# Last output chunk projected in two halves, with its own buffers and a second store queue, and the whole order planned anew

## The chip, the cores and the metric

The kernel runs on one core of a Trainium2 chip. The metric is the device time of one execution in microseconds (us). A core has five engines that each take their instructions in a fixed order: TensorE (PE, matmuls; its weight loads are listed as PEld), VectorE (DVE), ScalarE (ACT), GpSimd (POOL) and SyncE (SP, which here only issues DMAs). Engines wait for each other by semaphores. PSUM, where matmuls write, has eight banks of 512 fp32 columns.

## The reference

Block-sparse attention (4 batches, 8 heads, 768 positions, head size 64), and a gated long convolution on its output:

```
gate = q . mean of k over each block of 64;  keep the top 3 causal blocks and the own block
attn = softmax(q k^T / 8, kept blocks and causal) v          # per head
x    = heads side by side                                    # [4, 768, 512]
x1, x2, x3 = split(x @ w_proj)                               # w_proj [512, 1536]
c    = irfft(rfft(x2) * rfft(filter))                        # along the 768 positions
out  = (x1 * c * x3) @ w_out                                 # fp32 [4, 768, 512]
```

## The kernel before

Heads are taken in pairs: 16 groups g of two heads, four groups per batch. For each group `prep` transposes k and q on PE (L360, L424), copies them to SBUF (L373 on ACT, L427 on ACT), sums k blocks (L363 on DVE), computes gate scores (L483), the third largest (L493 to L500) and a block mask (L506, L528, L535; for later groups by DMA transposes L462 and L466). `attn` then computes scores in six pieces per group (L558, into two pairs of PSUM banks), exponentials (L565 on ACT), the causal triangle (L570 on POOL), the product with v (L588) and the division (L597, L601 on DVE). The result xn is transposed by DMA (L620) and transformed along the positions by matmuls (L638, L645; copied at L651).

For each batch b, when its four groups are done, `hyena` multiplies the transformed data by w_proj's second part (L747, called s2 here), by the filter's spectrum (L756 on DVE, L766 on POOL), transforms back (L810, copied at L819, combined at L825 on DVE), projects x1 and x3 (L783, called x13 here; x1 is copied by ACT at L789, x1*x3 is formed by DVE at L792), multiplies all (L831 on POOL, into yT), and projects with w_out: for each of six chunks of 128 positions four matmuls (L841), a copy to SBUF (L845, always on ACT in this order) and a store of 256 KB (L848, issued by SP).

The order of all instructions is not written by hand. `build` makes a graph of about 1,600 operations, each with a due time `vt` made of the numbers in `PAR`, and `plan` places them one by one on the engines with a table of costs, buffers (`POOLS`) and PSUM banks; among the operations that are ready within a small margin (`delta`) the earliest due time goes first. Until `warm_until` PE's idle places are filled with matmuls that nobody reads (L945, called fillers here). The result is one fixed list per engine. Any change of a cost, a due time or an operation's count can move everything that comes after.

Of the kernel before, what the change touches and what calls it, by code (L numbers as in the profile page):

```python
# [16 lines left out]
P = 128  # L17
NQ = S // P
NB = S // 64
NP = H // 2  # L20
NG = B * NP
Dm = H * D
# [22 lines left out]
for _pi, _segs in enumerate(PIECES):  # L45
    for (_col, _kc, _q0, _w) in _segs:
        for _c in range(_q0 // P, (_q0 + _w) // P):
# [1 line left out]


PAR = dict(
    direct=2, tm=9, kin=16, p0=-2.69, p1=0.365, pvlag=-6.582, dlag=1.76, dlen=1.383, h0=4.856,
    hlen=3.36, f0=-1.155, f1=7.084, ld=-3.238, s2a=-2.037, s2b=1.216, x0=0.354, x1=1.108, c0=-1.101,
    c1=2.132, o0=1.271, ahead=46.953, delta=0.033, queue=5.995, w0=1.489, wl=1.839, wlag=-9.917, warm_until=32.306,
    tr0=-18.919, trl=6.39, fill0=0.877, v_yT=7.627, v_sd=-1.517, d_k2=6.956, v_trig=-4.154, v_ldq=1.131, v_max=-5.158,
    v_g=0.972, v_Y=0.635, v_k2=0.499, v_rec=-6.814, v_small=-3.021, v_gate=0.152, v_km=0.106, d_x1=3.233, d_shQ=2.566,
    v_xT=-0.742, v_prod=-3.06, v_ldv=0.502, d_yT=8.721, v_ks=0.515, v_osb=-10.289, v_ldk=0.513, v_kT=0.073, v_gT=-1.053,
    d_md=-0.495, d_trig=6.615, v_qT=0.164, v_mT=0.152, v_lt=-2.205, v_fe=7.674, d_eo=-0.025, v_md=-2.102, v_phase=2.124,
    v_shQ=5.115, v_ldf=0.27, d_Y=3.198, v_sel=-7.798, v_warm0=4.967, v_x1=-4.181, v_ldw=0.046, v_tab=0.848, v_va=5.426,
    v_iota=-3.776, d_XT=-0.933, v_qh=0.379, v_h0=4.716, v_eblk=9.913, v_id32=-1.815, v_st=2.29, v_nyq=-4.563, v_s2=-2.561,  # L60
    v_st1=-0.047, v_XT=-3.549, v_t=-1.696, v_ql=-0.667, v_hf=-3.271, d_g=2.878, d_ce=12.21, d_osb=6.098, d_fill=0.038,
    v_w=-6.92, v_ce=0.546, v_fill=7.615, v_op=0.842, v_pv=-3.144, d_w=0.456, v_nrm=4.319, v_ha=-6.505, v_id16=4.506,
    v_eo=3.749, v_x13=-0.318, d_fe=-2.864, v_cv=-2.842, v_sc=0.099, v_T2=-3.366, v_T1=-1.079, d_qh=1.789, v_pq=-5.732,
    d_pq=12.199, v_ex=0.491, v_nid=0.437, a0=0.0, o1=1.0, pen_dve=0.205, late=2.0,
)

POOLS = dict(kn=2, qn=3, vn=2, k2=1, qx=4, ks=2, km=3, m8=2, gs=2, nm=1,
# [1 line left out]
             prod=3, ce=2, sd=2, yT=1, osb=4)  # L69


def c16(n):
    return max(0.026, n / 2400.0 + 0.0025)
# [14 lines left out]

class Graph:
    def __init__(self, par):  # L90
        self.ops, self.par = [], par

    def add(self, tag, vt, eng, emit, rd=(), wr=(), res=(), lock=False, size=0, quad=0):
        o = Op()
        vt += self.par.get("v_" + tag, 0.0)
        o.i, o.tag, o.vt, o.eng, o.emit, o.lock, o.size = len(self.ops), tag, vt, eng, emit, lock, size
        o.quad = quad
        deps = set()

        def norm(xs):  # L100
            return [x if isinstance(x, tuple) else (x, 0) for x in xs]

        bufs = []
        for b, p in norm(rd):
            deps.update(b.w.get(p, ()))
            b.r.setdefault(p, []).append(o)
            bufs.append(b)
        for b, p in norm(wr):
            deps.update(x for x in b.w.get(p, ()))
            deps.update(x for x in b.r.get(p, ()) if x is not o)  # L110
            b.w.setdefault(p, []).append(o)
            bufs.append(b)
        deps.discard(o)
        o.deps = list(deps)
        o.bufs = list({id(b): b for b in bufs}.values())
        for b in o.bufs:
            b.left += 1
        o.alloc = list({id(b): b for b in o.bufs + list(res)}.values())
        self.ops.append(o)
        return o  # L120


def pe_cost(mms):
    occ = sum(mms)
    return occ, occ + 0.23


def dve(n, rate=1.0):
    occ = n / (960.0 * rate) + 0.074
    return occ, occ + 0.15  # L130


def act(n, sb=False):
    occ = n / 1200.0 + 0.058 + (0.09 if sb else 0.0)
    return occ, occ + 0.165


def pol(occ):
    return occ, occ + 0.11


def build(par):
    g_ = Graph(par)
    add = g_.add
    C = {}

    def cb(name):
        if name not in C:
            C[name] = Buf(None)
        return C[name]  # L150

    def psb(n=1):
        return Buf("sp" if n == 2 else "bk")
# [4 lines left out]
    def e_id(E, nc, en):  # L158
# [4 lines left out]
        rd=[cb("id32")], wr=[cb("id16")])  # L163

    add("nid", T0 + 2.05, {"DVE": dve(64)}, lambda E, nc, en: nc.vector.tensor_scalar_mul(E.nid, E.id32, -float(S)),
        rd=[cb("id32")], wr=[cb("nid")], lock=True)
# [51 lines left out]
    for i in range(POOLS["kt"]):  # L218
# [5 lines left out]
        def e_fk(E, nc, en, i=i):  # L224
            eng = nc.vector if en == "DVE" else nc.gpsimd
            for h in range(2):
# [7 lines left out]
                rd=[cb("eblk")], wr=[(cb(("slot", i)), 1)], lock=True)])  # L234
# [13 lines left out]
    for t in range(HC):  # L248
        for hf in range(2):
            vt = par["tr0"] + par["trl"] * (0.33 * t + 0.16 * hf)  # L250
# [27 lines left out]

    kn, qn, va = {}, {}, {}
    for g in range(NG):  # L280
        b, j = divmod(g, NP)
        vt = g + par["ld"]
        kn[g], qn[g], va[g] = Buf("kn"), Buf("qn"), Buf("va")

        for n_, (src, dst) in enumerate((("k", kn[g]), ("q", qn[g]))):
            for t in range(2):
                def e_ld(E, nc, en, b=b, j=j, t=t, dst=dst, src=src, g=g):
                    nc.sync.dma_start(E.sb(dst)[:, :, 1 - t if src == "q" and g >= par["tm"] else t, :],
                                      getattr(E, src)[b, 2 * j + t].rearrange("(c p) d -> p c d", p=P))
                add("ld" + src, vt + .02 * n_ + .01 * t, {"SP": (0.5, 0)}, e_ld, wr=[(dst, t)], size=270)  # L290
        vn = Buf("vn")

        def e_lv(E, nc, en, b=b, j=j, vn=vn):
            s_ = E.v[b, 2 * j:2 * j + 2].rearrange("t (c p) d -> p (t c) d", p=P)
            nc.sync.dma_start(E.sb(vn), s_)

        def e_va(E, nc, en, vn=vn, va=va[g]):
            nc.gpsimd.affine_select(out=E.sb(va).rearrange("p t c d -> p (t c) d")[:, :, 0:D],
                                    in_=E.sb(vn), compare_op=ALU.is_ge, fill=0.0, base=0,
                                    pattern=[[0, 2 * NQ], [0, D]], channel_multiplier=0)  # L300

        add("ldv", vt + .6, {"SP": (0.55, 0)}, e_lv, wr=[vn], size=540)
        add("va", g + par["p0"] + 1.0, {"POOL": pol(0.86)}, e_va, rd=[vn, cb("small")], wr=[va[g]])

    fts = []
    for t in range(HC):
        f0, f1 = Buf("t"), Buf("t")
# [416 lines left out]
    def hyena(b):  # L724
        last = b == B - 1
        a, L = NP * b + par["h0"], par["hlen"]

        def v(f, lo=None, hi=None):
            if lo is not None:
                f = par[lo] + (par[hi] - par[lo]) * f  # L730
            return a + L * f
# [4 lines left out]
        for c in range(HC):  # L736
            for kind in range(2):
# [5 lines left out]
                def e_s2(E, nc, en, c=c, kind=kind, xa=xa):  # L743
# [8 lines left out]
                    wr=[xa], res=[ta, tb, Y])  # L752
                for i, dst in enumerate((ta, tb)):
                    def e_t(E, nc, en, c=c, kind=kind, i=i, dst=dst, xa=xa):
# [3 lines left out]
                        rd=[xa, (cb("HA"), c), (cb("HB"), c), cb("HA0")], wr=[dst])  # L758
            (t1, t4), (t3, t2) = ts[(c, 0)], ts[(c, 1)]
            for kind, (x, y, op) in enumerate(((t1, t2, ALU.subtract), (t3, t4, ALU.add))):  # L760
                for p_ in ((0,) if c < 2 else (0, 1)):
                    def e_y(E, nc, en, c=c, kind=kind, x=x, y=y, op=op, p_=p_):
# [6 lines left out]
                        rd=[x, y], wr=[(Y, (c, kind, p_))], lock=True)  # L769
        yT = Buf("yT")  # L770
        prods = {}
        for dc in range(NP):
            prod = prods[dc] = Buf("prod")
            for hf in range(2):
                cs = slice(HS * hf, HS * (hf + 1))
                x1 = Buf("x1")
                for m in range(2):
# [9 lines left out]
                    def e_xe(E, nc, en, cs=cs, m=m, xq=xq, x1=x1, prod=prod):  # L787
# [6 lines left out]
                    vt = v(f, "x0", "x1")  # L794
                    add("x13", vt, {"PE": pe_cost([c16(HS)] * 4)}, e_x,
                        rd=[xT[g] for g in gs] + [(cb(("wp", 2 * m)), c_) for c_ in range(NP)], wr=[xq], res=[x1, prod])
# [4 lines left out]
        for dc in range(NP):  # L801
            prod = prods[dc]
            ce, sd = Buf("ce"), Buf("sd")
            for p_ in range(2):
# [3 lines left out]
                def e_cv(E, nc, en, dc=dc, p_=p_, cv=cv):  # L808
# [4 lines left out]
                vt = v(f, "c0", "c1")  # L813
                need = [(Y, (p_, 0, 0)), (Y, (p_, 1, 0)), (Y, (2, 0, p_)), (Y, (2, 1, p_))]
                add("cv", vt, {"PE": pe_cost([c16(HS)] * 3)}, e_cv,
                    rd=need + [(cb("G"), 3 * p_ + n_) for n_ in range(3)], wr=[cv], res=[ce, sd, yT])
# [5 lines left out]
                else:  # L822
                    for i, op in enumerate((ALU.add, ALU.subtract)):
# [5 lines left out]
                        def e_yt(E, nc, en, i=i, dc=dc, sd=sd, prod=prod):  # L829
# [2 lines left out]
                                E.sb(yT)[:, dc, cs], E.sb(prod)[:, cs], E.sb(sd)[:, cs])  # L832
                        add("yT", vt + .04, {"POOL": pol(0.955), "DVE": dve(HS)}, e_yt, rd=[(prod, i), (sd, i)],
                            wr=[(yT, (dc, i))], lock=True)
        for c in range(NQ):
            op_, osb = psb(), Buf("osb")
            vt = v(c / 6.0, "o0", "o1")

            def e_op(E, nc, en, c=c, op_=op_):
                for d2 in range(NP):  # L840
                    nc.tensor.matmul(E.bk(op_), lhsT=E.sb(yT)[:, d2, P * c:P * (c + 1)], rhs=E.wo[:, d2, :],  # L841
                                     start=(d2 == 0), stop=(d2 == NP - 1))

            def e_os(E, nc, en, op_=op_, osb=osb):
                (nc.vector.tensor_copy if en == "DVE" else nc.scalar.copy)(E.sb(osb), E.bk(op_))  # L845

            def e_o(E, nc, en, c=c, osb=osb):
                nc.sync.dma_start(E.out[b, P * c:P * (c + 1), :], E.sb(osb))  # L848

            add("op", vt, {"PE": pe_cost([c16(Dm)] * 4)}, e_op,  # L850
                rd=[(yT, (d2, c // HC)) for d2 in range(NP)] + [(cb("wo"), c_) for c_ in range(NP)], wr=[op_], res=[osb])
            add("osb", vt + .02, {"ACT": act(Dm), "DVE": dve(Dm)}, e_os, rd=[op_], wr=[osb])
            add("st", vt + .04, {"SP": (0.5, 0)}, e_o, rd=[osb], size=262)


    for g in range(NG):
        C[("slots", g)] = Buf(None)
        C[("slots", g)].w[0] = sum(slot_init[:min(g + 1, POOLS["kt"])], [])
    for g in range(NG):
        prep(g)  # L860
    for g in range(NG):
        attn(g)
    filt()
    for b in range(B):
        hyena(b)
    return g_.ops

# [298 lines left out]
```

## Time and profile before

| | |
|---|---|
| median of 4 runs | 233.94 us (233.21 to 234.58) |
| profiled execution | 234.22 us, of which the span of the profile is 232.5 us |
| PE busy | 223.7 us (96%), 2189 matmuls, 116 of them fillers |
| DVE, ACT, POOL busy | 184.1, 176.0, 168.9 us |
| PE busy from 101 to 224 us | 123.00 of 123.00 us |
| last matmul ends | 228.8 us |
| last output copy | 228.89 us, 0.59 us long |
| last store issued | 229.5 us |
| stores, issue to landing | 2.0 us at least, 2.3 in the median |
| granted TensorE clock | 0.998 |

The page's rows name an engine, a line of the kernel, the operation and tiles as out<-in with partitions x elements; `x24 | 14.2, 590` means 24 instructions, 14.2 us busy in sum, 590 ns on the average. "idle before <-releaser" is the time for which the engine stood idle ahead of that group, and who ended it. Ends of matmuls are modelled, so a row of matmuls is better timed from start to start than by its end.

### The profile page before, as it was taken

Reading aid. Unit: us, or ns where it says so; the run is one execution under the profiler, and the core shown is the slowest. Engines: PE = TensorE matmul, PEld = TensorE weight load, DVE = VectorE, ACT = ScalarE, POOL = GpSimd, SP = SyncE. Lnnn points to the kernel's source line nnn. Section 1 sums busy time; section 2 is a strip of 40 time slices with the busy share of each in tenths; the row PEclk is TensorE's granted clock in tenths of the full one; section 3 lists DMA queues with packets and bytes.
Section 4 is the critical chain, followed back from the end, with each engine's and each line's share of the span. In section 5 each row is a group of like instructions: output and inputs, shape, how many; then the busy total and the mean of one; then the engine's idle time right before and its main releaser. Section 6 shows DMA issues by size and latency. Waiting matters only on the chain.

```text
span 232.5 us, 6222 instructions
## 1 busy us (share of the span) xinstructions
PE 223.7 (96%) x2189; PEld 151.4 (65%) x2189; DVE 184.1 (79%) x615; ACT 176.0 (76%) x295; POOL 168.9 (73%) x309
## 2 busy tenths in 40 slices
PE   8999999999897999999999999999999999999993
PEld 5787786767665677667655677676556667545551
DVE  7999779788987989998899597887987856594730
ACT  2988999999987798899957887999376675405343
POOL 8156467798669799979699999774598666069760
PEclk9999999999999999999999999999999999999999
DMA  7999999999999999999999999959912310512015
GB/s 157 330 223 202 218 176 233 231 209 253 180 218 234 220 213 200 222 252 223 174 227 215 284 190 226 174 98 178 259 52 79 70 34 3 171 45 90 3 45 226
DMA packets 120223, 40.91 MB, mean 176 GB/s; under 512 B 114304, under 2 KB 114304, under 8 KB 120192
## 3 DMA queue, kind: packets, MB, share of 16 engines
q1 hardware_dynamic: 120192, 40.51, 88.9%
q8 instruction: 17, 0.28, 0.6%
q14 instruction: 14, 0.11, 0.2%
HBM read 24.64 MB, written 6.29 MB: 133 GB/s over the span
## 4 chain that ended last, share of the span: by engine, by line
PE 63%; DVE 5%; DMA 4%; ACT 3%; issue 2%; SPq 1%; DVEq 0%; ACTq 0%
PE ps L783 15%; PE ps L558 10%; PE ps L841 9%; PE ps L747 7%; PE ps L588 6%; PE ps L810 6%; PE ps L638 4%; DMA t<-in_moe_w_proj_dram 2%; DMA kn<-in_k_dram 2%; PE ps L360 2%; PE ps L645 2%; ACT ex L565 2%; DVE ks L363 1%; PE ps L483 1%; DVE qx L457 1%
## 5 line engine op out<-in xcount | busy, mean ns | idle before, releaser
L565 ACT ACTIVATE ex<-ps 128x1024 f16<-128x1024 f32 (+1 forms) x96 | 86.4, 925 | 16.7 <-PE ps L558 16.1
L570 POOL TENSOR_SCALAR_AFFINE_SELECT ex<-ex 128x256 f16<-128x256 f16 x96 | 40.0, 424 | 23.3 <-ACT ex L565 21.5
L558 PE MATMUL ps<-qt,kt 76*128 76x512 f16 (+7 forms) x256 | 50.5, 305 | 1.2 <-ACT ex L565 0.7
L783 PE MATMUL ps<-xT,wp 128*128 128x384 f16 x256 | 49.8, 325 | 0.0
L766 POOL TENSOR_TENSOR Y<-t,t 128x512 f16<-128x512 f32 (+1 forms) x32 | 40.3, 1266 | 11.3 <-DVE t L756 10.2
L831 POOL TENSOR_TENSOR yT<-prod,sd 128x384 f16<-128x384 f32 x32 | 32.3, 1021 | 3.6 <-DVE sd L825 2.3
L373 ACT CAST kt<-ps 64x384 f16<-64x384 f32 x64 | 30.1, 472 | 6.1 <-PE ps L360 4.0
L558 PEld LDWEIGHTS <-kt 76*128 76x128 f16 (+1 forms) x256 | 23.5, 97 | 15.8 <-issue 1.8
L783 PEld LDWEIGHTS <-wp 128*128 128x128 f16 x256 | 24.1, 97 | 14.5 <-issue 0.3
L588 PEld LDWEIGHTS <-ex 128*128 128x128 f16 x672 | 25.5, 97 | 3.4 <-issue 1.0
L588 PE MATMUL ps<-va,ex 128*128 128x65 f16 x672 | 26.7, 193 | 0.5 <-DVE prod L792 0.3
L789 ACT CAST x<-ps 128x384 f16<-128x384 f32 x32 | 15.3, 478 | 14.0 <-PE ps L783 12.4
L792 DVE TENSOR_TENSOR prod<-ps,x 128x384 f32<-128x384 f32 x32 | 17.6, 552 | 8.6 <-PE ps L783 8.1
L841 PE MATMUL ps<-wo,yT 128*128 128x512 f16 x96 | 23.3, 379 | 0.0
L747 PE MATMUL ps<-wp,XT 128*128 128x512 f16 x96 | 22.5, 379 | 0.1
L845 ACT COPY osb<-ps 128x512 f32<-128x512 f32 x24 | 14.2, 590 | 8.2 <-PE ps L841 7.9
L651 DVE CAST XT<-ps 128x256 f16<-128x256 f32 (+1 forms) x30 | 16.1, 544 | 5.5 <-PE ps L645 3.6
L945 PE MATMUL ps<-warm 128*128 128x256 f16 x116 | 18.5, 296 | 1.1 <-DVE warm L1133 1.1
L810 PE MATMUL ps<-G,Y 128*128 128x384 f16 x96 | 19.0, 326 | 0.0
L363 DVE TENSOR_REDUCE ks<-ps 128x6 f32<-128x384 f32 x32 | 17.3, 547 | 2.2 <-ACT kt L373 1.4
L601 DVE TENSOR_TENSOR xn<-ps,rec 128x384 f16<-128x384 f32 x32 | 17.6, 551 | 0.7
L825 DVE TENSOR_TENSOR sd<-ce,ps 128x384 f32<-128x384 f32 x32 | 16.3, 546 | 1.6 <-ACT ce L819 1.5
(107 smaller groups left out, 376.8 us busy)
## 6 DMA issues: line engine op xcount, KB each, us to landing
kn<-in_k_dram SPq DMA_DIRECT2D x32, 192.0 KB, 4.4
vn<-in_v_dram SPq DMA_DIRECT2D x16, 384.0 KB, 5.5
qn<-in_q_dram SPq DMA_DIRECT2D x32, 192.0 KB, 4.5
out_dram<-osb SPq DMA_DIRECT2D x24, 256.0 KB, 2.3
t<-in_moe_w_proj_dram SPq DMA_DIRECT2D x12, 256.0 KB, 4.1
t<-in_moe_filter_fft_dram SPq DMA_DIRECT2D x6, 256.0 KB, 4.5
qt<-qx SPq DMA_DIRECT2D x14, 96.0 KB, 3.9
t<-in_moe_w_out_dram SPq DMA_DIRECT2D x4, 256.0 KB, 3.6
```

Source lines behind the costliest of these rows:

```text
L363: nc.vector.reduce_sum(E.sb(ks)[:, 6 * hf:6 * hf + 6], E.bk(kp)[:, 0:HS].rearrange("p (n t) -> p n t", t=64), axis=AX.X)
L373: (nc.scalar.copy if en == "ACT" else nc.vector.tensor_copy)(E.sb(Kt[g])[r, HC * hf:HC * (hf + 1), 1 - t, :], E.bk(kp)[r, 0:HS].rearrange( ...
L558: nc.tensor.matmul(o[:, col:col + w], lhsT=E.sb(Kt[g])[0:KR[t], kc, 1 - t, :], rhs=E.sb(Qt[g])[0:KR[t], q0 // P:(q0 + w) // P, 1 - t, :], ...
L565: nc.scalar.activation(E.sb(ex)[:, 0:w], E.sp(sp)[:, 0:w], AF.Exp, scale=ESC)
L570: nc.gpsimd.affine_select(out=dv, in_=dv, compare_op=ALU.is_ge, fill=0.0, base=0, pattern=[[0, 2], [1, P]], channel_multiplier=-1)
L588: nc.tensor.matmul(o[:, 65 * c:65 * c + 65], lhsT=E.sb(exs[pi])[:, col:col + P], rhs=E.sb(va[g])[:, t, kc, :], start=(kc == 0), stop=(kc = ...
L747: nc.tensor.matmul(E.bk(xa), lhsT=w, rhs=E.wp[:, j, Dm:2 * Dm], start=(j == 0), stop=(j == NP - 1))
L766: (nc.vector if en == "DVE" else nc.gpsimd).tensor_tensor(E.sb(Y)[ro, n_, :], E.sb(x)[ri, :], E.sb(y)[ri, :], op=op)
L783: nc.tensor.matmul(E.bk(xq)[:, 0:HS], lhsT=E.wp[:, d2, 2 * Dm * m + P * dc:2 * Dm * m + P * (dc + 1)], rhs=E.sb(xT[gs[d2]])[:, cs], start= ...
L810: nc.tensor.matmul(E.bk(cv)[:, 0:HS], lhsT=E.sb(Y)[:, 3 * p_ + n_, P * dc:P * (dc + 1)], rhs=E.G[:, 3 * p_ + n_, :], start=(n_ == 0), stop ...
L831: (nc.vector if en == "DVE" else nc.gpsimd).tensor_mul(E.sb(yT)[:, dc, cs], E.sb(prod)[:, cs], E.sb(sd)[:, cs])
L841: nc.tensor.matmul(E.bk(op_), lhsT=E.sb(yT)[:, d2, P * c:P * (c + 1)], rhs=E.wo[:, d2, :], start=(d2 == 0), stop=(d2 == NP - 1))
```

## The change

The output projection of the last batch is rewritten. Chunks 0 to 4 remain four matmuls of 512 columns, one copy and one store of 256 KB. Chunk 5 becomes two operations of 256 columns each, with four matmuls, one copy and one store of 128 KB apiece; the store of the second half is issued by ACT (`nc.scalar.dma_start`) instead of SP. In the last batch chunks 4 and 5 are copied into buffers of the pool `prod`, not of `osb`. The chunks' due times in the last batch follow the order 0 to 5, where the order before came out as 2, 1, 5, 4, 3, 0.

`Graph` can now add a number per operation and group to the due time (`v_<tag>_<group>`), some 390 such numbers are set, and most of the old numbers in `PAR` have other values. `POOLS` and the cost functions are as before. So the plan comes out differently on every engine.

```diff
@@ PAR
-    direct=2, tm=9, kin=16, p0=-2.69, p1=0.365, pvlag=-6.582, dlag=1.76, dlen=1.383, h0=4.856,
+    direct=2, tm=9, kin=16, p0=-2.688, p1=0.365, pvlag=-7.248, dlag=1.795, dlen=1.312, h0=4.884,
...
+    d_pq=12.713, v_ex=0.48, v_nid=0.704, v_va_0=0.132, v_ldq_1=-0.543, v_ldq_2=1.495, v_ldv_3=0.132, v_ldk_4=-0.165, v_ldq_4=-0.2,
...
@@ class Graph
-        self.ops, self.par = [], par
+        self.ops, self.par, self.group = [], par, -1
...
         vt += self.par.get("v_" + tag, 0.0)
+        if self.group >= 0:
+            vt += self.par.get("v_%s_%d" % (tag, self.group), 0.0)
@@ hyena
-        for c in range(NQ):
-            op_, osb = psb(), Buf("osb")
-            vt = v(c / 6.0, "o0", "o1")
+        for c, n0, n1 in [(c, 0, Dm) for c in range(NQ - last)] + [(NQ - 1, 0, 256), (NQ - 1, 256, Dm)] * last:
+            op_, osb, n = psb(), Buf("prod" if last and c >= 4 else "osb"), n1 - n0
+            vt = v(0.0, "o0", "o1") + 0.01 * (c + n0 / Dm) if last else v(c / 6.0, "o0", "o1")
...
-                    nc.tensor.matmul(E.bk(op_), lhsT=E.sb(yT)[:, d2, P * c:P * (c + 1)], rhs=E.wo[:, d2, :],
-                                     start=(d2 == 0), stop=(d2 == NP - 1))
+                    nc.tensor.matmul(E.bk(op_)[:, 0:n1 - n0], lhsT=E.sb(yT)[:, d2, P * c:P * (c + 1)],
+                                     rhs=E.wo[:, d2, n0:n1], start=(d2 == 0), stop=(d2 == NP - 1))
...
-                (nc.vector.tensor_copy if en == "DVE" else nc.scalar.copy)(E.sb(osb), E.bk(op_))
+                (nc.vector.tensor_copy if en == "DVE" else nc.scalar.copy)(E.sb(osb)[:, 0:n], E.bk(op_)[:, 0:n])
...
-                nc.sync.dma_start(E.out[b, P * c:P * (c + 1), :], E.sb(osb))
+                (nc.scalar if n0 else nc.sync).dma_start(E.out[b, P * c:P * (c + 1), n0:n1], E.sb(osb)[:, 0:n1 - n0])
...
-            add("op", vt, {"PE": pe_cost([c16(Dm)] * 4)}, e_op,
+            add("op", vt, {"PE": pe_cost([c16(n)] * 4)}, e_op,
...
-            add("osb", vt + .02, {"ACT": act(Dm), "DVE": dve(Dm)}, e_os, rd=[op_], wr=[osb])
-            add("st", vt + .04, {"SP": (0.5, 0)}, e_o, rd=[osb], size=262)
+            add("osb", vt + .02, {"ACT": act(n), "DVE": dve(n)}, e_os, rd=[op_], wr=[osb])
+            add("st", vt + .04, {"SP": (0.5, 0)}, e_o, rd=[osb], size=262 * n // Dm)
...
     for g in range(NG):
+        g_.group = g
         prep(g)
     for g in range(NG):
+        g_.group = g
         attn(g)
+    g_.group = -1
     filt()
     for b in range(B):
+        g_.group = b
         hyena(b)
```

What the plan makes of it, read from the two built programs: PE's list is the same for its first 283 matmuls (the profile before has the 283rd at 32 us) and has one filler more (117); its score pieces then stand at the same place, counted in PE's work, to within 1.5 us until piece 63 of 96, and drift up to 4.6 us from there. SP's list differs first at its fourth issue: the first two filter loads go ahead of both halves of the first q load, where they stood between the halves. ACT's list differs first after 52 instructions. All copies of output chunks stay on ACT.

## The prediction

> **What bounds the kernel now.** I read the page's first part, then PE by stretches, then the stretches where it idles, then the end. The page says that PE is the bound:
>
> ```profile
> PE 223.7 (96%) x2189; PEld 151.4 (65%) x2189; DVE 184.1 (79%) x615; ACT 176.0 (76%) x295; POOL 168.9 (73%) x309
> ```
>
> An average hides where the 4% lie, so the next view is busy time by stretches. Look at the PE column only:
>
> ```profile
> core 0: us, PE busy (x) PEld busy (x) DVE busy (x) ACT busy (x) POOL busy (x), PEclk, DMA share, GB/s
> 33.00:60.00 27.00, 25.75 (x336) 19.17 (x335) 22.92 (x102) 26.67 (x44) 20.28 (x46) 1.00 1.17 221
> 60.00:80.00 20.00, 17.61 (x198) 11.90 (x197) 17.60 (x62) 16.98 (x28) 15.92 (x30) 1.00 1.18 208
> 95.00:101.00 6.00, 5.67 (x55) 3.87 (x54) 5.71 (x20) 4.86 (x9) 5.00 (x9) 1.00 1.31 206
> 101.00:224.00 123.00, 123.00 (x1150) 79.46 (x1148) 97.29 (x294) 84.51 (x136) 93.54 (x157) 1.00 0.69 141
> 224.00:229.00 5.00, 4.81 (x23) 1.98 (x21) 0.28 (x1) 3.04 (x6) 1.05 (x2) 1.00 0.49 188
> ```
>
> From 101 to 224 us PE never idles, and the clock is full. No order can be faster there, only slower. What an order can win lies at 33 to 101 us: 1.25 + 2.39 + 0.33 = 4.0 us by these rows. Ends of matmuls are modelled, so busy time swallows short waits. Counted from start to start (24 matmuls of 512 columns in 5.18 us, so 216 ns each; 16 of 384 columns in 2.60 us, 163 ns each) PE loses 7.8 us there, spread over two dozen places of 0.1 to 0.85 us. The largest cluster:
>
> ```profile
> 71.27 1.02 PE L747 MATMUL ps<-wp,XT 128*128 128x512 f16 x4
> 72.99 0.85 PE L360 MATMUL ps<-id,kn 128*128 128x128 f32 x6 [0.69 <-DMA kn<-in_k_dram]
> 75.74 0.44 PE L528 MATMUL ps<-id,nm 128*128 128x128 f16 x5 [0.65 <-DVE ks L363]
> 76.57 1.02 PE L747 MATMUL ps<-wp,XT 128*128 128x512 f16 x4
> ```
>
> A load of k is late by 0.7 us, then a PSUM bank that DVE still reads, by 0.65. The end is short:
>
> ```profile
> 223.45 5.36 PE L841 MATMUL ps<-wo,yT 128*128 128x512 f16 x24
> 228.03 0.59 ACT L845 COPY osb<-ps 128x512 f32<-128x512 f32 x1 [0.32 <-PE ps L841]
> 228.89 0.59 ACT L845 COPY osb<-ps 128x512 f32<-128x512 f32 x1 [0.28 <-PE ps L841]
> DMA to landing us min/median/max: 2.0/2.3/4.7
> ```
>
> 24 projection matmuls end at 228.81, the last copy runs to 229.48, its store is issued at 229.5 and lands 2.0 us later, and 1.0 us of closing work ends the span at 232.5. Only these 3.7 us after the last matmul belong to the edit that can be read in the diff.
>
> **The change part by part**, against the profiled execution (234.22 us, span 232.5, so 1.72 around it). It lies 0.28 above the median of 233.94, and the sum is lowered by that at the end.
>
> *The tail.* Eight matmuls of 256 columns replace four of 512: three of 256 take 0.33 us elsewhere (L638, 109 ns each), so 8 x 109 = 872 against 4 x 216 = 864 ns: nothing. Copies cost by size:
>
> ```profile
> L845 ACT COPY osb<-ps 128x512 f32<-128x512 f32 x24 | 14.2, 590 | 8.2 <-PE ps L841 7.9
> L819 ACT COPY ce<-ps 128x384 f32<-128x384 f32 x16 | 7.6, 479 | 3.3 <-DVE sd L825 1.6 <-PE ps L810 1.5
> ```
>
> 128 columns less save 111 ns, so 256 columns take some 368 ns. But chunk 4's copy and both halves stand one after the other on ACT: chunk 4 from 228.03 to 228.62, the first half, ready at 228.46, until 228.99, the second, ready at 228.89, until 229.36 instead of 229.48. That is -0.12, not -0.22. The last store moves 128 KB instead of 256. No row shows a lone store of that size; at the most that any slice of the page moved (330 GB/s) the missing 128 KB are 0.4 us, at least they are nothing; I take -0.2. That ACT issues it removes a hop of 0.02 us (copy end to SP's issue). ACT's queue is not used before; SP's stores took 332 to 1301 ns to issue, so this costs nothing to +0.97, and I take nothing, since that queue is empty. Nothing is queued behind it on ACT. Tail: -0.3, ends -0.5 to +0.85.
>
> The row that bears on it: a store of 256 KB lands here 2.0 us after its issue. The page "DMA: Bandwidth & Descriptors" of the Trainium skill speaks against this part. Under "Anatomy of one DMA" (written of GpSimd's path) it gives a DMA about 2.0 us whatever its size plus its bytes at 436 GB/s, 2.6 us for such a store, and under "Rules for kernel authors" it says that spreading DMAs over several issuing engines saves only issue time. By it the half store would gain an estimated 0.3 us and the second queue no more than an issue; the sum would then be 0.1 us lower.
>
> *Own buffers, chunk order.* A copy reuses the first of four `osb` buffers four chunks (4 x 0.86 = 3.4 us) later, and its store has landed 0.59 + 2.05 us after that copy began: no wait before, none to win. The `prod` buffers' last readers are multiplies (L831) that PE must await anyway. Chunks 0, 1, 2 first means that the second half of yT is wanted one chunk later. PE idles 0.19 us in 224 to 229: -0.1, ends -0.19 and 0.
>
> *The plan, 0 to 33 us.* PE's list is the same. The first q half is issued two places later, but q's transpose needs both halves, and the second keeps the seventh place: nothing. The one added filler (109 ns) comes just ahead of PE's waits for exponentials: covered; 0.11 if that cover is gone.
>
> *33 to 60 us.* ACT is busy 26.67 of 27.00 us. The new order swaps copies with exponentials (up to 1.1 us of ACT work either way) but has the same ACT work ahead of exponential 24, so the stretch ends with ACT: 0, ends -0.33 and +0.5 (half the largest swap, if ACT is then starved once).
>
> *60 to 80 us.* PE's list is the same up to the gate after L528. The late k load keeps its place behind the same issues (the transpose of xn goes ahead of three issues that it followed): its 0.7 us stay. Then ACT's list changes: a weight cast (L322, 0.61) moves ahead of three k copies (L373, 0.47 each), and an exponential goes behind that cast and one more copy. The mask transpose (L528) now waits for x1's copy in its bank, which ends after two casts, two k copies and itself: 73.62 + 2 x 0.61 + 3 x 0.47 = 76.25 instead of 75.74. Then the second matmul group of s2 (0.86 us) is pulled forward to where x13 had waited, and by score piece 37 I come to 81.2 us with 0.3 us less work done, against 81.54 before. +0.1; ends -1.1 (the 0.65 and, from start to start, 0.30 and 0.19 behind it gone) and +1.1 (the ACT work that now stands ahead of the exponential).
>
> *95 to 101 us.* Same PE and DVE lists; one k copy goes behind an exponential. 0, end -0.33.
>
> *101 to 224 us.* Much is moved: batch 0's projection comes together, k transposes go 11 us later, loads change places with stores on SP. SP's queue is where stores wait for ACT with loads behind them. Counting PE work between producer and consumer, the transposed scores' masks (gate to scores) get more room (10.5 us at least before, 13.5 now), the filter products 5.6 to 6.3, the multiplies ahead of w_out about the same. Closer are bank waits on DVE in batch 1: one x13 group loses 1.7 us of PE work ahead of it while the L825 that frees its bank gets 2.1 us more DVE work; the timeline has 3.4 us of room there, so -0.4. With DVE at 97 of 123 us I take +0.3. It can't be below 0; the upper end is 2.4, what PE lost in 60 to 80, the worst stretch that this planner left.
>
> Sum: -0.3 - 0.1 + 0 + 0 + 0.1 + 0 + 0.3 = 0.0, so 234.2 for an execution like the profiled one and **233.9** for the median. A comparison of this kernel can tell about 0.5% from no change, 1.17 us: same means 232.8 to 235.1.
>
> **The rivals.** *New waits in the dense part (slower).* The place is 110 to 195 us, where the new order differs most; the mechanism is a matmul that waits for DVE or POOL to free a bank. For it: DVE is at 97 of 123 us and 33 to 101 us shows that such plans do leave such waits. Against it: the distances above. Four waits of the 0.65 seen at L528 are 2.6 us: 233.94 + 2.6 - 0.4 = 236.1. It decides from 1.6 us of new PE idle on.
>
> *The early waits close (faster).* If the three waits from L528 on go (1.1) and half the 0.33 at 95 to 101, with the tail's 0.4 and no new wait: 233.94 - 0.4 - 1.1 - 0.2 = 232.2. For it: 4.0 us of idle PE. Against it: the lists there are nearly the same, and two of the causes are untouched.
>
> *The split does nothing.* The halves' copies queue on ACT and the landing is latency: then the tail gives 0.1 and the time is 234.1, inside the forecast's class.
>
> **How the numbers follow.** Forecast, the split's failure with it: 0.57. Slower by the rival: 0.23. Faster: 0.20. The forecast's own range is 232.8 to 235.1; to hold 8 in 10 it reaches about half into each rival: 232.3 to 235.6.
>
> **What would show it.** Right: PE busy within 0.5 us of 123 between 101 us and the last 5 us; the last copies near 0.37 us each; from the last matmul to the span's end 3.4 us. Wrong: idle PE over 1.5 us after 101 us; PE's wait at L528 gone; a last store that lands over 2.3 us after its issue.

## The result: 0.5% slower, and the profile after

| | before | after |
|---|---|---|
| median of all runs | 233.84 us (68 runs) | 235.12 us (42 runs) |
| ratio to the kernel before, 95% interval | 1 | 1.0051 (1.0039 to 1.0064) |
| profiled execution, and its span | 234.22, 232.5 us | 235.40, 233.7 us |
| last matmul starts / last store lands | 228.43 / 231.56 us | 229.83 / 232.74 us |

The forecast was "same", 233.9 us. The measured time lies inside the range of 232.3 to 235.6, but the change is 1.2 us in the direction that was given 0.23.

The same view as before, busy time by stretches, shows where PE stands idle now (first number: length; second: PE busy; then PEld, DVE, ACT, POOL, PEclk):

```profile
33.00:60.00 27.00, 24.84 (x336) 19.13 (x333) 22.28 (x100) 26.70 (x44) 21.93 (x49) 1.00 1.19 219
60.00:80.00 20.00, 17.39 (x188) 11.64 (x185) 17.16 (x62) 16.24 (x28) 15.76 (x27) 1.00 1.07 207
95.00:101.00 6.00, 5.72 (x58) 4.02 (x56) 5.71 (x21) 5.22 (x10) 5.15 (x9) 1.00 1.29 188
101.00:124.00 23.00, 23.00 (x221) 14.56 (x219) 20.89 (x69) 17.69 (x28) 18.95 (x40) 1.00 1.20 236
124.00:132.00 8.00, 6.90 (x94) 5.25 (x93) 6.98 (x13) 5.58 (x10) 6.77 (x13) 1.00 1.10 242
132.00:225.00 93.00, 93.00 (x837) 59.43 (x836) 72.71 (x216) 59.65 (x98) 66.00 (x104) 1.00 0.58 107
```

Ahead of 101 us the picture is nearly the old one: from 33 to 60 us PE is busy for 0.9 us less, but counted from start to start (the time between two matmul starts, less what the first needs) it lost the same there to within 0.2 us. Behind it PE was full before; now 1.10 us are missing from 124 to 132 us, and nowhere else. The view of PE's waits from 100 to 140 us has a single line for the kernel after, and none for the kernel before (us in total, times, longest):

```profile
PE ps L686 <- DVE eo L674: 1.1, 1, 1.1
```

PE's timeline around that place:

```profile
126.38 0.50 PE L408 MATMUL ps<-id,kn 128*128 128x128 f32 x3
127.98 0.50 PE L686 MATMUL ps<-F,eo 128*128 128x256 f16 x3 [1.10 <-DVE eo L674]
```

From start to start it is 1.27 us. L686 is the transform of group 8's xn along the positions; it reads `eo`, the sum and the difference of xn's halves, made by DVE. DVE's timeline, and then POOL's, say why `eo` is late:

```profile
123.47 0.55 DVE L649 TENSOR_TENSOR xn<-ps,rec 128x384 f16<-128x384 f32 x1
124.64 0.56 DVE L411 TENSOR_REDUCE ks<-ps 128x6 f32<-128x384 f32 x1 [0.62 <-PE ps L408]
125.11 1.47 DVE L505 SCALAR_TENSOR_TENSOR qx<-qn,qx 128x640 f16<-128x640 f32 x1
126.51 1.89 DVE L674 TENSOR_TENSOR eo<-xn 128x384 f16<-128x384 f16 x2
129.25 0.67 DVE L699 CAST XT<-ps 128x512 f16<-128x512 f32 x1
```

```profile
125.12 0.78 POOL L618 TENSOR_SCALAR_AFFINE_SELECT ex<-ex 128x256 f16<-128x256 f16 x2
125.99 1.72 POOL L814 TENSOR_TENSOR Y<-t,t 64x512 f16<-64x512 f32 x1
```

Two things are to be seen. The order: xn comes at 123.47, behind a block of twelve filter products (L804, from 115.95 to 123.55), where the kernel before had it at 116.26, in front of them. DVE's rows of the kernel before:

```profile
116.26 0.56 DVE L601 TENSOR_TENSOR xn<-ps,rec 128x384 f16<-128x384 f32 x1
122.31 1.79 DVE L457 SCALAR_TENSOR_TENSOR qx<-qn,qx 128x640 f16<-128x640 f32 x1
124.03 0.55 DVE L626 TENSOR_TENSOR eo<-xn 128x384 f16<-128x384 f16 x1
130.17 0.20 DVE L597 RECIPROCAL rec<-ps 128x6 f32<-128x6 f32 x1 [2.19 <-PE ps L483]
```

And the durations: the two `eo` take 1.89 us, qx 1.47, while the views of single lines give these spreads over the kernel (ns, least/median/most):

```profile
L674 DVE TENSOR_TENSOR eo<-xn x19: 341/354/1443, 62.0 to 200.4; 128x384 f16<-128x384 f16 x19
```

```profile
L505 DVE SCALAR_TENSOR_TENSOR qx<-qn,qx x7: 817/925/1470, 91.0 to 160.7; 128x640 f16<-128x640 f32 x7
```

```profile
L840 DVE TENSOR_TENSOR prod<-ps,x x32: 537/552/559, 84.8 to 225.0; 128x384 f32<-128x384 f32 x32
```

eo and qx read two operands from SBUF, and their longest take 4 and nearly 2 times as long as their shortest; prod reads one of its two from PSUM and does not vary. The first eo (126.51 to 127.92) ends 0.2 us after POOL's Y ends (127.71), and Y itself takes 1.72 us instead of 1.29 (the Y before it): it is recorded from 125.99, while qx ran until 126.58. By these rows each holds the other up; for eo, run 2 below tests it.

The Trainium skill's page "SBUF — State Buffer", section "Who interferes with whom", says that a VectorE instruction with two SBUF inputs contends with a GpSimd instruction that reads SBUF, and that the ports which the two engines share are an exclusive lock. These rows agree: the long eo lasted until Y had ended.

The end of the kernel by the timeline, ACT's copies and the issues of the stores, and then the copies by their line:

```profile
229.32 1.25 ACT L894 COPY prod<-ps 128x512 f32<-128x512 f32 x3 [0.33 <-PE ps L890]
229.93 0.81 SPq L898 DMA_DIRECT2D out_dram<-prod  x2
230.60 0.38 ACTq L898 DMA_DIRECT2D out_dram<-prod  x1
```

```profile
L894 ACT COPY prod<-ps x3: 372/377/586, 229.3 to 230.2; 128x256 f32<-128x256 f32 x2, 128x512 f32<-128x512 f32 x1
```

The copies are 0.37 us long, as forecast. ACT's store is issued at 230.60 and lands at 232.74, 2.14 us later; the whole chunk took 2.06.

### The profile page after: what moved, and what is told of

The parts are those of the page before. It is cut to its first block, busy times and chain, and to the rows that moved or that the text cites. A ratio compares the mean times of both kernels' runs of the same rounds, so it can differ in the third digit from the quotient of the medians.

```text
span 233.7 us, 6234 instructions
## 1 busy us (share of the span) xinstructions
PE 222.1 (95%) x2194; PEld 151.0 (65%) x2194; DVE 186.7 (80%) x616; ACT 174.8 (75%) x296; POOL 168.6 (72%) x308
## 4 chain that ended last, share of the span: by engine, by line
PE 67%; ACT 11%; DMA 8%; DVE 6%; issue 3%; POOL 2%; SPq 1%; DVEq 0%; ACTq 0%
PE ps L831 15%; PE ps L606 9%; PE ps L890 9%; PE ps L795 7%; PE ps L858 6%; PE ps L636 6%; ACT ex L613 5%; DMA kn<-in_k_dram 4%; DMA xT<-xn 4%; PE ps L686 3%; ACT kt L421 3%; PE ps L999 3%; PE ps L408 2%; PE ps L693 2%; ACT qx L475 1%
## 5 line engine op out<-in xcount | busy, mean ns | idle before, releaser
L831 PEld LDWEIGHTS <-wp 128*128 128x128 f16 x256 | 24.1, 97 | 13.8
L837 ACT CAST x<-ps 128x384 f16<-128x384 f32 x32 | 15.4, 480 | 13.4 <-PE ps L831 12.5
L890 PE MATMUL ps<-wo,yT 128*128 128x512 f16 (+1 forms) x100 | 23.5, 370 | 0.0
L411 DVE TENSOR_REDUCE ks<-ps 128x6 f32<-128x384 f32 x32 | 17.4, 548 | 4.4 <-PE ps L408 2.4
L894 ACT COPY osb<-ps 128x512 f32<-128x512 f32 x22 | 12.9, 585 | 10.1 <-PE ps L890 10.0
L804 DVE TENSOR_TENSOR t<-ps,HA 128x512 f32<-128x512 f32 x24 | 16.4, 683 | 2.4 <-PE ps L795 2.2
```

What stands on the lines that cost most here:

```text
L831: nc.tensor.matmul(E.bk(xq)[:, 0:HS], lhsT=E.wp[:, d2, 2 * Dm * m + P * dc:2 * Dm * m + P * (dc + 1)], rhs=E.sb(xT[gs[d2]])[:, cs], start= ...
L890: nc.tensor.matmul(E.bk(op_)[:, 0:n1 - n0], lhsT=E.sb(yT)[:, d2, P * c:P * (c + 1)], rhs=E.wo[:, d2, n0:n1], start=(d2 == 0), stop=(d2 == ...
```

## The experiments

The theory to be tested: the 1.2 us are lost by PE at 124 to 132 us to DVE, and the tail is worth about 0.1 us. Rivals: the tail itself costs the time; or the new order is tight in many places, so that no single wait can be blamed. In most runs the planned order of the kernel after is kept and a few operations are moved by hand: `move` takes the named operations (tag and running number in the graph; group 8 has eo16 and eo17) out of the list and puts them elsewhere, so that all other instructions keep their places. Of the tags, `sel` is a triangle mask and `Y` a product on POOL; `ql` is qx, `nrm` xn, `t` a filter product and `XT` a copy on DVE; `T` is the DMA transpose of qx's result, and `ldk` a load of k.

### 1. eo ahead of qx on DVE

```diff
     order = plan(PAR)
+    order = move(order, ["eo16", "eo17"], ahead="ql21")
```

> The kernel after, with two instructions of DVE's list moved: group 8's sum and difference (eo, L674) go ahead of the qx instruction (L505) that stood before them. One-wait theory: the 1.2 us are PE's wait at 128 us for these two eo; they now begin at 125.1 instead of 126.5 and end before PE wants them at 126.9, the wait goes, PE loses nothing in 124 to 132 us, and the time falls by 1.0 to 1.3 to about 233.9, ratio to the kernel before 1.000 (0.998 to 1.002). Spread theory (the new order is tight everywhere): another wait of 0.5 us or more comes up behind it and the ratio stays at 1.003 or more. Tail theory (the halves and ACT's queue cost it): nothing changes, 1.005.

Measured: 1.0070 (1.0047 to 1.0092). PE's wait for eo was gone, the time was not. In the profiled execution PE's clock was at half for 3.4 us from 58.3 us on (rows in the last section), and at 111 us PE was 1.6 us later than in the kernel after, so this profile says little by itself. But 8 of the 12 executions had a granted clock of 0.999 or more, and their median is 235.7 us too. It was run again (5).

### 2. Y two places later on POOL

```diff
+    order = move(order, ["Y13"], behind="sel59")
```

> The kernel after, with one instruction of POOL's list moved: the product Y (L814, 1.72 us long) that began at 125.99 goes behind the two triangle masks (L618) that followed it. DVE's and PE's lists stay. If an eo with both operands in SBUF is held by a long POOL instruction beside it (eo took 1.41 us there, 0.35 in the median, and ended 0.2 us after Y), the first eo now takes 0.35 to 0.5 us, both end at 127.2 or before instead of 128.0, PE's wait shrinks from 1.1 to 0.2 to 0.5 us, and the ratio to the kernel before falls from 1.005 to about 1.002. If eo is slow for a reason of its own (its place behind qx), it still takes over 1 us and the ratio stays at 1.005. If the tail makes the loss, 1.005 as well, but with the short eo.

Measured: 1.0016 (0.9994 to 1.0038); 234.61 us, against 235.34 for run 3 on the same chip, which has the same order without this move. The interval lies just below that of the kernel after (1.0039 to 1.0064) and overlaps that of run 3. DVE's timeline, and then POOL's:

```profile
124.62 1.47 DVE L505 SCALAR_TENSOR_TENSOR qx<-qn,qx 128x640 f16<-128x640 f32 x1
126.01 0.61 DVE L674 TENSOR_TENSOR eo<-xn 128x384 f16<-128x384 f16 x2
```

```profile
124.64 0.77 POOL L618 TENSOR_SCALAR_AFFINE_SELECT ex<-ex 128x256 f16<-128x256 f16 x2
128.26 1.27 POOL L814 TENSOR_TENSOR Y<-t,t 64x512 f16<-64x512 f32 x1
```

No instruction of DVE or PE was touched, and the two eo, with nothing of POOL beside them, take 0.61 us instead of 1.89. qx stays at 1.47: the two masks still run beside it. PE's wait fell from 1.27 to 0.20 us, and another of 0.31 us appeared at 135.7 us. What a DVE instruction costs is decided here by what POOL does beside it.

### 3 and 4. The tail undone, and the tail alone

Run 3 is the kernel after with the last chunk whole:

```diff
             def e_op(E, nc, en, c=c, op_=op_, n0=n0, n1=n1):
+                if n0:
+                    return
+                n1 = Dm
...  (the same in e_os and e_o: the first half does the whole chunk, the second nothing; SP stores)
```

> The kernel after with its order, but with the last chunk whole again: four matmuls of 512 columns, one copy, one store of 256 KB by SP (own buffers and chunk order stay). One-wait theory: the wait at 128 us stays and the tail is worth 0.1 us (from the last matmul's start to the span's end 4.07 us before and 3.88 after, less 0.11 of matmul length), so 235.2 to 235.4, ratio 1.0055 to 1.0065. The prediction's tail of -0.3: 235.4. Tail theory: the loss goes, 233.9, ratio 1.000.

Run 4 is the kernel before, in its own order, with its last chunk in halves:

```diff
+                if b == B - 1 and c == 0:
+                    for n0, s_ in ((0, op_.slot), (256, E.other)):
+                        for d2 in range(NP):
+                            nc.tensor.matmul(E.ps[:, 512 * s_:512 * s_ + 256], lhsT=E.sb(yT)[:, d2, 0:P],
+                                             rhs=E.wo[:, d2, n0:n0 + 256], start=(d2 == 0), stop=(d2 == NP - 1))
+                    return
...
+                    nc.sync.dma_start(E.out[b, 0:P, 0:256], E.t["prod"][2][:, 0:256])
+                    nc.scalar.dma_start(E.out[b, 0:P, 256:Dm], E.t["prod"][0][:, 0:256])
```

> The kernel before with its order, with the new tail alone: its last chunk projected, copied and stored in halves, the second half's store by ACT's queue. One-wait theory: -0.1 us, ratio 0.9995 (0.998 to 1.001). The prediction's tail: -0.3, ratio 0.9987. Tail theory: +1.2, ratio 1.005.

Measured: run 3 1.0053 (1.0028 to 1.0078), run 4 1.0004 (0.9977 to 1.0030). Neither moves its kernel measurably: the tail is not the cause. The profiles give its worth, from the end of the last matmul (its start plus 216 or 109 ns) to the landing of the last store: 2.91 us before and 2.90 in run 3 (whole), 2.80 after and 2.81 in run 4 (halves). That is 0.1 us.

### 5. The kernel after, and run 1, once more

> The kernel after once more, as the yardstick for the others. One-wait theory: the wait of 1.1 to 1.3 us for eo at 128 us is in this profile too, since nothing random stands ahead of it, and the ratio to the kernel before is 1.005 (1.003 to 1.007). If the wait was an accident of one execution, PE loses under 0.5 us between 124 and 132 us here.

> The first experiment (eo ahead of qx on DVE) once more. Its profile had PE's wait at 128 us gone, but 1.7 us more lost ahead of 101 us, where its instructions are those of the kernel after, and a granted clock of 0.97 and 0.96 from 33 to 80 us. One-wait theory with a disturbed first run: ratio 0.999 to 1.002, no PE loss in 124 to 132 us, and 11.5 to 12.5 us lost ahead of 101 us by the stretches (PE start to start) instead of 13.6. If the move itself costs time, the ratio is again 1.005 or more.

Measured: the kernel after 1.0044 (1.0017 to 1.0071), run 1's edit 1.0058 (1.0029 to 1.0087). The loss is in the kernel after's second profile too (0.85 us in front of L693, which reads the second eo). With eo moved ahead it is not gone but elsewhere; PE's waits from 100 to 140 us in that run:

```profile
PE ps L831 <- DVE prod L840: 0.4, 1, 0.4
PE ps L831 <- DVE XT L699: 0.3, 1, 0.3
```

These are banks that DVE frees later. Y now runs beside qx and not beside eo, and it is qx that is long, as DVE's and POOL's timelines show:

```profile
126.45 1.90 DVE L505 SCALAR_TENSOR_TENSOR qx<-qn,qx 128x640 f16<-128x640 f32 x1
126.40 1.27 POOL L814 TENSOR_TENSOR Y<-t,t 64x512 f16<-64x512 f32 x1
```

In run 1's first profile the Y's fell otherwise (125.55 to 126.81, and from 128.00), and qx took 1.02 us. So the one-wait theory falls in its first form: eo was only the first to be late in a row of DVE instructions that is late as a whole. What fits is the length of that row, from the start of ks (L411) to the end of the copy XT (L699): 5.28 us in the kernel after (124.64 to 129.92), 5.28 in run 3, 4.92 in the second run of the kernel after, 4.93 here, 4.01 in run 2, 3.85 in run 1. PE lost, from start to start, 1.3, 1.3, 0.95, 0.95, 0.5 and 0.0 us in the stretch.

### 6. Both moves

```diff
+    order = move(order, ["eo16", "eo17"], ahead="ql21")
+    order = move(order, ["Y13"], behind="sel59")
```

> The kernel after with both moves: eo ahead of qx on DVE, and the product Y behind the two masks on POOL. One-wait theory: PE loses nothing in 124 to 132 us, 0.2 us less than with Y's move alone, ratio 0.999 to 1.002. Spread theory: 1.003 or more.

Measured: 1.0029 (0.9998 to 1.0059), which lies between the two theories. The row is 3.85 us, as in run 1, where PE lost nothing in the stretch; here it lost 0.2 us at 132 and 0.3 us at 138 us.

### 7. A shorter row

```diff
+    order = move(order, ["Y13"], behind="sel59")
+    order = move(order, ["ql21", "T13"], behind="XT16")
```

> The kernel after with DVE's row of work at 125 to 130 us made shorter: the product Y behind the two masks on POOL, and qx (L505, with the transpose of its result that SP issues) behind the copy XT (L699) on DVE. DVE-row theory: what PE loses there is how long DVE takes from the sum ks to the copy XT, beyond some 3.9 us (row 5.28, 4.93, 4.01 and 3.85 us, PE's loss 1.31, 0.95, 0.2 and 0.0 to 0.2 in the runs so far), whatever stands in which place. The row is now 2.9 to 3.3 us, PE loses nothing from 124 to 140 us, and the ratio to the kernel before is 0.999 to 1.001, 1.0 us under the kernel after. Spread theory: another wait of 0.5 us or more appears behind and the ratio stays at 1.003 or more.

Measured: 1.0052 (1.0028 to 1.0076). The row was 3.63 us (over what was expected, as DVE now had gaps in it) and PE ran through 124 to 132 us without a gap. Then two waits came, of 0.53 and 0.47 us from start to start. PE's waits from 100 to 140 us:

```profile
PE ps L858 <- POOL Y L814: 0.4, 1, 0.4
PE ps L831 <- DVE sd L873: 0.3, 1, 0.3
```

The Y that was moved back is now late itself. The spread theory was right here.

### 8 and 9. xn and eo earlier, by two and by eight products

```diff
+    order = move(order, ["nrm17", "eo16", "eo17"], ahead="t22")     # run 9: ahead="t16"
```

> The kernel after, with three instructions of DVE moved: group 8's last xn (L649) and the two eo made from it go ahead of the last two filter products (L804 of t22 and t23), which they had followed. Nothing is moved on POOL and PE. Lost-room theory: the new order put xn and eo behind a block of twelve filter products, so that eo is made 1.4 us before PE wants it (it was made 9 us before in the kernel before). Then DVE's row from ks to the copy XT falls from 5.28 to 4.0 to 4.3 us, PE loses 0.1 to 0.5 us from 120 to 140 us instead of 1.3, and the ratio to the kernel before falls from 1.005 to 1.000 to 1.002. Full-engines theory (DVE and POOL have no room at all from 116 to 137 us, as the moved waits of the ninth run say): the loss comes up for another product, 0.9 to 1.3 us, and the ratio stays at 1.004 to 1.006.

> The same three instructions six filter products earlier, ahead of t16 (118.7 us), right when xn's sums are there. Lost-room theory: eo is ready 7 us before PE wants it, the row as in the run beside it, loss 0.0 to 0.5 us, ratio 0.999 to 1.002. Full-engines theory: the products Y that POOL makes from the later filter products are late instead, loss 0.9 us or more for the transforms back (L858), ratio 1.004 to 1.006.

Measured: 1.0067 (1.0039 to 1.0094) and 1.0133 (1.0097 to 1.0168). PE's longest wait of the stretch in run 8, and then in run 9:

```profile
PE ps L831 <- DVE t L804: 1.0, 1, 1.0
```

```profile
PE ps L795 <- DVE t L804: 1.9, 1, 1.9
```

The filter products also free the PSUM banks that PE needs next; whatever is put ahead of them, PE waits for them instead. In run 9 a second price came on top, the clock. Run 9 by stretches around that wait (last numbers: PEclk, DMA share, GB/s):

```profile
116.00:120.60 4.60, 4.60 (x41) 2.42 (x39) 3.95 (x11) 1.15 (x2) 2.68 (x5) 1.00 1.04 276
120.60:123.10 2.50, 0.64 (x5) 0.33 (x4) 2.50 (x4) 1.02 (x1) 0.99 (x1) 1.00 1.21 276
124.40:128.00 3.60, 3.60 (x11) 1.37 (x10) 2.19 (x4) 2.27 (x3) 3.60 (x5) 0.53 1.07 223
128.00:132.00 4.00, 4.00 (x39) 2.96 (x38) 2.38 (x4) 3.72 (x7) 2.57 (x4) 1.00 1.18 242
```

Some 1.9 us without work, and for 3.6 us PE gets half its clock: 11 matmuls where 39 run in 4 us afterwards (of other sizes; consecutive ones of 512 columns start 0.43 us apart instead of 0.216).

### 10. Both halves stored by SP

```diff
-                (nc.scalar if n0 else nc.sync).dma_start(E.out[b, P * c:P * (c + 1), n0:n1], ...)
+                nc.sync.dma_start(E.out[b, P * c:P * (c + 1), n0:n1], ...)
```

> The kernel after with the second half's store issued by SP as well. The prediction (ACT's queue costs nothing): the last store lands 2.0 us after its issue, and from the last matmul's start to that landing 2.9 us as with ACT. If ACT's queue is the slower one (2.14 us from issue to landing in the kernel after, against 1.98 for the half that SP issues): the issue comes 0.15 us later, behind the first half's, the landing 0.15 us sooner after it, and the sum is the same within 0.05 us. If two halves in one queue get in each other's way, it lands 0.2 us or more later.

Measured in one profiled execution: issues at 230.61 and 231.10, the last landing at 232.98, 1.88 us after its issue. From the last matmul's start (230.09) to that landing it is 2.89 us, with ACT's queue 2.91. By these two executions the second queue is worth 0.02 us: what it saves in issue time its store takes longer to land.

### 11 to 13. Versions meant to beat both kernels

Runs 11 and 12 are run 4 (before with the new tail) with two k loads moved up in SP's list; run 13 is run 7 with the same.

```diff
+    order = move(order, ["ldk15"], behind="ldk14")     # runs 12 and 13: ahead="shQ10"
+    order = move(order, ["ldk17"], behind="ldk16")
```

> A candidate to beat both: the kernel before with the new tail, and two loads of k moved up in SP's list (group 7's second half right behind its first, group 8's second half right behind its first; they were issued at 58.8 and 67.8 us, landed 5.1 us later, and PE waited 0.63 and 0.85 us for them). If these loads are what PE lacks there, both waits go, with them part of the 0.8 us wait behind them, and the tail gives 0.1: ratio 0.992 to 0.996. If the DMA engines, saturated there, only pass the delay on to the next load, a wait of the same size comes up for another load and the ratio is 0.999 to 1.001.

> The second try at beating both: the kernel before with the new tail and the two k loads moved up, but group 7's second half now goes behind two loads of w_proj that it had overtaken (overtaking them made POOL's casts, and behind them a triangle mask, late: PE waited 0.9 us for that mask at 62.6). If that was the only new wait, PE's lines lose about 1 us less from 60 to 67 us than with the first try, both waits for k stay away, and the ratio to the kernel before is 0.992 to 0.996. If the DMA engines are simply full there, another load is late by 0.5 us or more and the ratio is 0.998 to 1.000.

> The same and two loads of k moved up in SP's list (group 7's second half behind the loads of w_proj that it follows no longer by an xT and two q transposes, group 8's second half behind its first). The kernel after waits 0.95 us at 64.0 and 0.97 us at 73.1 for them. If the waits go as they did in the kernel before (0.5 us less lost by 101 us there, though the time showed nothing), the ratio is 0.995 to 0.999; if other loads are late in their place, 0.999 to 1.001.

Measured: 0.9985 (0.9956 to 1.0014), 0.9996 (0.9973 to 1.0019) and 1.0057 (1.0032 to 1.0082). PE's waits for k at 64 and 73 us went in runs 11 and 12. In run 11 POOL's triangle mask was late instead, as PE's timeline shows:

```profile
62.61 1.04 PE L588 MATMUL ps<-va,ex 128*128 128x65 f16 x19 [0.90 <-POOL ex L570]
```

In run 12 smaller waits took their place (0.25 to 0.33 us, four of them from 61 to 66 us). Neither is faster than the kernel before by more than its interval, so no version here beats it. Run 13 keeps run 7's losses behind 120 us (1.1 us) and with them its ratio.

### All profiles side by side

Loss is from start to start, in PE's own work: "early" is all that PE lost until 100 us of its work were done (with the 1.12 us ahead of its first matmul), "dense" what it lost in the next 40 us of work. Each is one execution. What a matmul needs enters the early column: with the median of each shape in the kernel before it would be 2.7 us higher in every row, and the differences between rows stay.

| kernel | ratio | early | dense |
|---|---|---|---|
| before | 1 | 12.3 | 0.0 |
| 4 before, new tail | 1.0004 | 12.0 | 0.0 |
| 11, 12 before, new tail, k earlier | 0.9985, 0.9996 | 12.7, 11.8 | 0.0, 0.1 |
| after, twice | 1.0051, 1.0044 | 12.0, 13.4 | 1.3, 0.95 |
| 3 after, old tail | 1.0053 | 11.9 | 1.3 |
| 2 after, Y later | 1.0016 | 11.5 | 0.5 |
| 6 after, both moves | 1.0029 | 13.8 | 0.5 |
| 1 after, eo first, twice | 1.0070, 1.0058 | 13.6, 12.3 | 0.0, 0.95 |
| 7, 13 after, shorter row | 1.0052, 1.0057 | 12.2, 11.9 | 1.1, 1.1 |
| 8, 9 after, xn earlier | 1.0067, 1.0133 | 13.4, 12.7 | 1.3, 3.7 |
| 10 after, both halves by SP | not measured | 12.6 | 0.95 |

The early column differs by over 1 us between executions of one kernel; the dense column is near zero for everything in the old order and about 1 us for nearly everything in the new one, and the ratios follow it, with run 1 as the exception, the first above all. Part of that lies in where the columns meet. From 88 to 100 us of PE's work (some 102 to 115 us of the profile), where the kernel before lost 0.1 us, run 1 lost 0.7 and 0.6 us in its two profiles, and runs 6 and 10 lost 0.4; the other profiles of the new order lost under 0.1. With it run 1's second profile lost 1.6 us in the dense part, more than the kernel after, as its ratio says. Run 10 has the planned order on DVE and POOL, so the moves need not be the reason; it stays open.

## Why the prediction was wrong

**The step that failed is the term "101 to 224 us: +0.3".** It measured +1.3 in the first profile of the kernel after and +0.95 in the second, both behind 124 us, and 0.1 more at 165 us in each. Two things went into it. First, the dependences that the prediction names (masks, filter products, multiplies, bank waits) do not include group 8's eo. The first of the pair had moved from POOL to DVE; in the kernel before the pair was made 9 us before PE wanted it, and in the new order it lay right in front of its use. Second, DVE was priced at its share of busy time ("DVE at 97 of 123 us"), while the trace of before already held a qx of 1.79 us beside a Y and a mask of POOL, where others took 0.81. In the kernel before that long qx made PE wait for nothing, and DVE stood idle for 2.19 us soon after (at 128 us); in the new order DVE has one gap over 0.2 us from 116 to 130 us, of 0.62 us.

**The rival on the slower side came true in place and kind, at half its price.** It named 110 to 195 us and a matmul that waits for DVE or POOL. The first wait was not for a bank but for an operand, though after run 1's move and in runs 8 and 9 it was banks. Its price, four waits of 0.65 us, was 2.6 us; measured was one row that is 1.3 us too long. "It decides from 1.6 us of new idle on" was close: 1.3 us of loss gave 235.12, at the edge of what was called the same (235.1).

**The tail was mis-sized: -0.3 forecast, -0.1 measured.** The copies were right (0.37 us) and did not even queue, so that the last one ended 0.2 us sooner after the last matmul than before. But the landing term of -0.2 was +0.08: half the bytes land no sooner (2.14 us after the issue, against 2.06), and in SP's queue 1.88.

**Right steps.** From 0 to 33 and 33 to 101 us nothing was to change by more than 0.1: the loss until 100 us of work is 12.3 before, 12.0 and 13.4 after, with other executions of either order in between. The mask transpose was to start at 76.25 us, waiting for x1's copy on ACT, and the two waits behind it were to go; its row, from PE's timeline, shows that wait, and those behind it are gone:

```profile
76.24 0.44 PE L576 MATMUL ps<-id,nm 128*128 128x128 f16 x5 [1.01 <-ACT x L837]
```

That the time agrees to 0.01 us is luck: in the second profile of the kernel after the same row starts at 77.65 us, in run 1's second at 75.97. The two waits for k stayed (0.79 and 0.81 us, against 0.46 and 0.69 by the same kind of row).

**The account of the 1.2 us**, from the two profiled executions: loss from start to start +1.17 (dense +1.31, early -0.28, behind it +0.14), one more filler +0.11, tail -0.1: 1.18, against spans of 233.7 and 232.5.

**What stays open.** That Y on POOL holds eo on DVE, and that this makes most of the wait, is shown by run 2 (one POOL instruction moved, 0.8 us less lost by PE). The time agrees, 0.7 us less than run 3, but the intervals of the two ratios overlap, so the gain in time is less sure than the cause. That a smaller edit could win it all back is not: in the profiles nearly every other move passed the wait to the next user of DVE, to a bank or to POOL's Y. Which of the 390 new due times crowd that stretch was not tried one by one. Nor is it known why PE lost another 0.4 to 0.7 us at 102 to 115 us in four of the twelve profiles of the new order.

## What to carry to other kernels

When a scheduler replans everything, compare for each operand the time between its making and its use, and look first at those whose maker has changed its engine; and price instructions by the longest time that the trace shows for them, not the mean, where a neighbour can hold them. Where an engine has next to no idle time over a stretch, moving one instruction in it mostly changes who waits, as in runs 1, 7, 8 and 9; what helped here was less holding by the neighbour (run 2). A second store queue and half the bytes buy little where 128 KB take 1.9 to 2.1 us to land and 256 KB 2.1: 0.1 us here, all of it from the shorter copy.

## What the runs showed of the hardware

Two points were not expected. A DVE instruction with two SBUF operands is recorded as long as it was held: the same eo took 0.34 us alone, 0.55 us where a mask on POOL (0.42) had begun just before it, and 1.41 us beside a Y.

And PE's clock fell to half after short pauses. After waits of 1.98 us (run 8) and 1.86 us (run 9) the granted clock was 0.50 and 0.53 in stretches of 3.2 and 3.6 us that begin some 1.4 us behind the wait. Run 8 by stretches, the wait in the first row:

```profile
73.80:76.20 2.40, 0.42 (x7) 0.24 (x5) 0.86 (x3) 2.36 (x6) 2.33 (x2) 1.00 0.76 96
77.40:80.60 3.20, 3.20 (x10) 1.34 (x9) 3.12 (x18) 1.03 (x3) 2.70 (x7) 0.50 0.87 220
```

In run 1's first profile two shorter waits did the same, of 0.82 and 0.81 us (0.98 and 0.97 from start to start), the second ending 1.2 us after the first; they lie in the first row:

```profile
54.50:58.30 3.80, 2.17 (x28) 1.66 (x26) 2.77 (x19) 3.33 (x6) 3.11 (x7) 1.00 1.20 241
58.30:61.70 3.40, 3.40 (x36) 2.99 (x35) 1.48 (x6) 2.57 (x4) 2.51 (x5) 0.50 1.47 220
```

The same two waits in the second profile of the kernel after (0.91 and 0.80 us) left the clock at 1.00, and so did single waits of up to 1.48 us (run 9, at 57.6 us). So the length of a wait alone does not decide; what else does is not shown by these runs. Over whole executions, a granted clock of 0.993 or less stands in 3 of 54 of the kernel after, and in none of 127 of the kernel before measured beside runs 1 to 13. These are too few to make the difference of the medians.

The Trainium skill's page "TensorE: Matmul & The Clock Gate", section "HAM oscillation — how this bites in real kernels", gives as the rule that pauses over about 3.4 us are to be avoided. Here the measurement decides: one pause of 1.9 us was enough, and once two of 0.8 us close together.
